# A two-layer expert kernel: the first and last step of layer two on all eight banks, weight sums spread over other ticks, and a fixed order for the matrix engine

## The chip, the cores and the metric

One core of one Trainium2 chip runs the kernel. The metric is the device time of one launch in microseconds (us). The matrix engine is PE, its weight loads PEld; VectorE is DVE, ScalarE ACT, GpSimd POOL, and SP is the engine that issues most DMA transfers.

## The reference

Linear attention feeds a feed-forward layer with ELU (layer one), and that a mixture of four experts with ReLU (layer two). 2304 tokens, width 512, all in float32:

```
kv  = einsum('bhsd,bhse->bhde', k, v);  o = einsum('bhsd,bhde->bhse', q, kv)
x   = o / sqrt(mean(o*o) + 1e-6) * g_norm              # 2304 x 512
h   = x @ w_in;  y = elu(h) @ w_out                    # layer one, 512 -> 2048 -> 512
p   = domain_probs / (sum(domain_probs) + 1e-9)
out = sum over e of p[:, e] * (relu(y @ w1[e]) @ w2[e])   # layer two, 512 -> 1024 -> 512
```

## The kernel before

**Numbers.** w_in and w_out arrive as float64 bit patterns and are turned into float32 on DVE and ACT (`convert`, in five pieces). Every large product is made of three passes: each operand is split into a high part (a cast on ACT, lines 194, 266 and 638) and a low part (a subtraction, line 191 or 271, on POOL or DVE), and PE multiplies high by high, high by low and low by high. A matmul has 128x128 weights and 384 tokens.

**Layer one.** Tokens go in six blocks of 384 (T), hidden units in 16 chunks of 128, taken in the groups 0-1, 2-3, 4-7, 8-11 and 12-15. Group one is computed inside the attention, block by block (index j). One chunk and one block is 12 matmuls into bank `ps_h` (`product1`, lines 481 to 483), ELU (`begin_elu` on ACT, `end_elu` at line 495 on DVE, which frees the bank), a split (`split_h`), and 12 matmuls into the four banks `ps_y` (`product2`, lines 513 to 515), which DVE or ACT adds into `acc` (line 507, line 505). There are two `ps_h` banks, so `product1` of one chunk waits until line 495 has read the chunk two before.

**Layer two.** Tokens go in three pairs of blocks, with four experts each: twelve steps (`moves`). Each step multiplies by blocks 2x2 in Strassen's manner with seven products, P1 to P7: a q half (x by w1) and an m half (hidden by w2), each of 7 products by two slices s, so 14 units of 12 matmuls. q units of step n alternate with m units of step n-1. In the first step there are only q units, and behind the last q unit only m units of the last step. Line 576 is every matmul of both halves. Results lie in four double banks: `qa` and `qb` for q, `ma` and `mb` in turn for m. P2 goes into the bank of P1 and P6 into that of P5 once ACT has copied it (`copy p`, line 692, line 601 for q); DVE adds the banks into sums u and c (lines 604 to 620 and 697 to 713). The hidden blocks are added up (`sums_of_h`, lines 628 to 630), cast (line 638) and lowered (line 191); results are weighted (line 684) and added into `acc` (line 685). At the end of a pair 128x128 transposes on PE turn `acc` (`emit_out`, line 731), ACT copies them and a DMA stores them. Halfway through the last step of a pair `make_forms` adds up the next pair's x blocks (line 327). All the tiles that hold these intermediate results come in turn from one ring of 16 (`small`).

**Weights of layer two.** The 16 quarters of w1 and w2 are loaded in blocks b11 to b22 (`load_block`, line 248), added into t1 to t4 (line 261, DVE), split and written back to memory (`keptw`, line 276). Three tables say at which tick of its quarter each piece starts: `FORMS_SLOW`, `FORMS_FAST` and `FORMS_LATE`; a b entry loads a block of the next quarter, and the number behind the table is the length of a quarter in ticks. Twelve quarters are made during layer one, four in layer two. A tick is one turn of the loop that writes the program, 12 matmuls.

**Order.** The attention runs in a hand-written order on every engine (a place number for each piece; `at_place`). From the last three groups of layer one on, DVE, ACT and POOL run in the order of the program (`in_program_order`), while PE and SP run in the order that a scheduler chose. On SP all loads and stores stand in one queue: a store that waits for its data holds up the loads behind it.

## Time and profile before

| | before |
|---|---|
| median of three runs (lowest to highest) | 1195.65 us (1195.27 to 1197.15) |
| the profiled execution, its own time | 1193.98 us |
| its span in the trace | 1192.2 us |
| PE busy | 1166.6 us, 98% of the span |
| DVE, POOL, ACT busy | 799.4, 676.0, 587.3 us |

The profile is one execution. Its time is 1.67 us below the median, and 1.78 us of it lie outside the span. PE's share is an average over stages, so that the idle time of PE has to be looked for stage by stage: 0 to 115 us attention with group one, to 465 us the other groups of layer one, to 494 us the first step of layer two, from 1148.35 us the m units of the last step.

### The profile page before, as it was taken

The page shows a single profiled execution, that of the slowest core. Times are in us where ns is not written, and L with a number is a line of the kernel's source. Part 1 is how long each engine was busy: PE and PEld are TensorE (multiplying, and loading weights), DVE is VectorE, ACT ScalarE, POOL GpSimd, SP SyncE. Part 2 cuts the span into 40 slices and gives each one's busy share as a digit, 9 for nine tenths or more (in the row PEclk, how much of TensorE's full clock was granted, in tenths as well). Part 3 has the DMA queues.
Part 4 walks back from the last instruction along what each step waited for, and adds up shares of the span by engine and source line. Part 5 has one row for each costly group of instructions (what it writes and reads, how often), then busy time and mean ns, then how long its engine had stood idle before and what let it go on. Part 6 is the DMA issues. An engine that isn't in the chain of part 4 may idle for free.

```text
span 1192.2 us, 18877 instructions
## 1 busy us (share of the span) xinstructions
PE 1166.6 (98%) x7039; PEld 1151.9 (97%) x7039; DVE 799.4 (67%) x945; ACT 587.3 (49%) x937; POOL 676.0 (57%) x526
## 2 busy tenths in 40 slices
PE   9899999999999999999999999999999999999997
PEld 8899999999999999999999999999999999999996
DVE  5877987767776673667687956364758573647485
ACT  3677656666665563544444443434344434343342
POOL 1223457777777693676678954454567544445441
PEclk9999999999999999999999999999999999999999
DMA  9614777668778866999998978888888888888873
GB/s 344 231 44 142 256 262 250 228 219 314 244 219 291 314 249 219 347 332 367 319 352 305 346 245 256 284 252 267 247 274 257 260 265 273 262 259 267 257 242 114
DMA packets 112159, 312.22 MB, mean 262 GB/s; under 512 B 19580, under 2 KB 40644, under 8 KB 110532
## 3 DMA queue, kind: packets, MB, share of 16 engines
q1 hardware_dynamic: 106372, 296.86, 74.4%
q10 hardware_dynamic: 5696, 14.16, 3.3%
q8 instruction: 56, 0.92, 0.3%
q14 instruction: 35, 0.29, 0.1%
HBM read 238.06 MB, written 72.91 MB: 261 GB/s over the span
## 4 chain that ended last, share of the span: by engine, by line
PE 55%; DVE 3%; issue 1%; ACT 0%; POOL 0%; ACTq 0%; DVEq 0%; POOLq 0%
PE ps_qb L576 16%; PE ps_ma L576 15%; PE ps_mb L576 13%; PE ps_qa L576 11%; DVE acc L685 1%; DVE m L684 0%; PE ps_mb L731 0%; DVE h L629 0%; DVE h L191 0%; DVE u L604 0%; DVE h L628 0%; POOL c L707 0%; DVE u L704 0%; DVE f L191 0%; PE ps_ma L731 0%
## 5 line engine op out<-in xcount | busy, mean ns | idle before, releaser
L191 POOL TENSOR_TENSOR h<-h 128x384 fp32r<-128x384 f32 x232 | 284.0, 1250 | 203.8 <-ACT h L638 198.3
L576 PE MATMUL ps_qb<-f,ws 128*128 128x384 f32 x1152 | 216.9, 336 | 4.8 <-DVE u L604 3.7
L576 PEld LDWEIGHTS ps_qb<-f,ws 128*128 128x128 f32 x1152 | 201.1, 188 | 6.1 <-DVE u L604 4.7
L576 PE MATMUL ps_ma<-h,ws 128*128 128x384 f32 x1080 | 200.0, 335 | 0.8 <-DVE h L191 0.7
L191 POOL TENSOR_TENSOR h<-e,h 128x384 fp32r<-128x384 f32 x93 | 107.5, 1157 | 149.1 <-ACT h L194 135.2
L576 PEld LDWEIGHTS ps_ma<-h,ws 128*128 128x128 f32 x1080 | 187.9, 188 | 1.9 <-DVE h L191 1.0
L576 PE MATMUL ps_mb<-h,ws 128*128 128x384 f32 x936 | 173.5, 336 | 1.6 <-ACT o L738 0.8
L638 ACT CAST h<-h 128x768 fp32r<-128x768 f32 x168 | 139.9, 833 | 66.9 <-PE ps_ma L576 35.9
L576 PEld LDWEIGHTS ps_mb<-h,ws 128*128 128x128 f32 x936 | 164.1, 189 | 2.2 <-issue 1.1
L576 PE MATMUL ps_qa<-f,ws 128*128 128x384 f32 x864 | 162.7, 334 | 0.5 <-DVE acc L507 0.5
L576 PEld LDWEIGHTS ps_qa<-f,ws 128*128 128x128 f32 x864 | 150.7, 188 | 1.1 <-DVE acc L507 0.9
L595 ACT ACTIVATE h<-h 128x768 f32<-128x768 f32 x72 | 61.0, 848 | 154.9 <-DVE h L610 73.2
L481 PE MATMUL ps_h<-x,w 128*128 128x384 f32 x384 | 129.7, 338 | 4.7 <-DVE e L495 4.7
L482 PE MATMUL ps_h<-x,w 128*128 128x384 f32 x384 | 128.6, 335 | 0.7 <-DVE x L457 0.7
L515 PE MATMUL ps_y<-h,w 128*128 128x384 f32 x384 | 128.4, 334 | 0.7 <-POOL w L191 0.7
L514 PE MATMUL ps_y<-h,w 128*128 128x384 f32 x384 | 128.4, 334 | 0.2 <-POOL h L191 0.2
L483 PE MATMUL ps_h<-x,w 128*128 128x384 f32 x384 | 128.4, 334 | 0.0
L513 PE MATMUL ps_y<-h,w 128*128 128x384 f32 x384 | 122.2, 336 | 0.2 <-ACT acc L505 0.2
L495 DVE SCALAR_TENSOR_TENSOR e<-e,ps_h 128x384 f32<-128x384 f32 x96 | 52.6, 549 | 68.6 <-ACT e L491 58.0
L271 POOL TENSOR_TENSOR wform<-wform 128x512 fp32r<-128x512 f32 x56 | 81.2, 1458 | 24.1 <-ACT wform L266 17.4
L194 ACT CAST h<-e 128x384 fp32r<-128x384 f32 x96 | 49.0, 511 | 68.0 <-DVE e L495 67.9
L490 ACT ACTIVATE e<-ps_h 128x384 f32<-128x384 f32 x96 | 46.9, 489 | 66.3 <-PE ps_h L483 58.3
(119 smaller groups left out, 1870.8 us busy)
## 6 DMA issues: line engine op xcount, KB each, us to landing
ws<-keptw SPq DMA_DIRECT2D x336, 512.0 KB, 4.5
keptw<-wform SPq DMA_DIRECT2D x112, 512.0 KB, 4.2
wraw<-in_moe_w_dram SPq DMA_DIRECT2D x64, 256.0 KB, 5.5
keptx<-x ACTq DMA_DIRECT2D x6, 1536.0 KB, 6.5
x<-keptx SPq DMA_DIRECT2D x6, 1536.0 KB, 8.6
raw<-in_moe_w_in_dram SPq DMA_DIRECT2D x16, 512.0 KB, 4.2
raw<-in_moe_w_out_dram SPq DMA_DIRECT2D x16, 512.0 KB, 4.4
qkv<-in_k_dram SPq DMA_DIRECT2D x18, 256.0 KB, 5.8
```

The source lines that it names most:

```text
L191: eng.tensor_tensor(out=l, in0=x, in1=h, op=ALU.subtract)
L271: eng.tensor_tensor(out=f[:, 1].bitcast(F32R), in0=src, in1=f[:, 0], op=ALU.subtract)
L481: nc.tensor.matmul(ps, ah, bh, start=(kk == 0), stop=False)
L482: nc.tensor.matmul(ps, ah, bl, start=False, stop=False)
L483: nc.tensor.matmul(ps, al, bh, start=False, stop=(kk == KD - 1))
L495: nc.vector.scalar_tensor_tensor(out=e, in0=e, scalar=-1.0, in1=ps_h.pop((j, c)), op0=ALU.add, op1=ALU.max)
L513: nc.tensor.matmul(ps, bh[:, cols], hi, start=first, stop=False)
L514: nc.tensor.matmul(ps, bh[:, cols], lo, start=False, stop=False)
L515: nc.tensor.matmul(ps, bl[:, cols], hi, start=False, stop=last)
L576: nc.tensor.matmul(ps[:, c, :T], a, x[:, b, kk, :], start=start and kk == 0 and n == 0, stop=stop and kk == 1 and n == 2, skip_group_check ...
L595: nc.scalar.activation(src, src, AF.Relu)
L638: nc.scalar.copy(f[:, 0], src)
```

## The change

**Attention.** The low parts of the first block's h and of the first two chunks of w_out move from POOL to DVE. In block 1 both halves of the first `half` (24 matmuls) stand before the 12 transposes of the next x, where one half stood; the ELU of chunk 0 of block 1 comes later.

**Conversions.** Those of group one come every 3.4 ticks instead of every 3, the later ones start 3 ticks later.

**Weight sums.** Quarters of `FORMS_SLOW` last 12 ticks, not 13, and there are 8 of them, not 7; those of `FORMS_FAST` last 10, not 8, and there are 4, not 5. In the fast table the block b21 of the next quarter is loaded 4 ticks before its use in t4, where it was 2 (from tick 10 to tick 14, where it was 9 to 11). `FORMS_LATE` starts at tick 10, lasts 26.

**Orders.** SP runs in program order in the last three groups, PE in program order in layer two.

**First step.** Its products come as P1 P3 P2 P5 P4 P6 P7 and take the four double banks in turn.

**Small tiles.** Weighted results are multiplied in place instead of into a new tile, and the sums of the last pair's x blocks lie in an `acc` tile that is free by then.

**Last step.** Its 14 m units come in an order of their own, P1 P3 P5 P3 P5 P4 P2 P6 P7 with slices mixed, on all banks. Eight of its operands are split ahead into the place of x blocks that are no longer needed; for slice 1, and for S2 and A22, DVE makes the low parts. The last quarter of the output is transposed and added up on PE: `add_third` multiplies by the identity into a bank, first `acc`, then the weighted last product, in three thirds that ACT copies and SP stores.

```
-    FORMS_SLOW = "t1:0 t2:2 P5:3 t3:4 t4:5 P3:6 b12:7 b11:7 P4:7 ... P6:11 b21:12", 13
-    FORMS_FAST = "t1:0 t2:1 P5:2 t3:2 b12:3 b11:3 b22:3 t4:3 ... P6:9 b21:9", 8
+    FORMS_SLOW = "t1:0 t2:2 P5:3 t3:4 b12:5 b11:5 t4:5 P3:6 P4:7 ... P6:11 b21:11", 12
+    FORMS_FAST = "t1:0 t2:1 P5:2 t3:3 b12:4 b11:4 t4:4 P3:5 b22:5 ... P6:10 b21:10", 10
...
-            d["a"] = double("qa")
+            d["a"] = next_m(ALL) if step == moves[0] else double("qa")
...
-        on_vector = a in ("S2", "A22") or step == moves[-1] and a in ("A12", "S4")
+        on_vector = a in ("S2", "A22") or step == moves[-1] and s and a != "A11"
...
-        m = small("m")
+        m = src if last_use else small("m")
         tt(out=m, in0=src, in1=by, op=ALU.mult)
...
+            transposed = out_part(p, 0, 1)
+            by, t = late["p", step][:, 1, :], small("m")
+            for n, m in enumerate(thirds):
                 tt(out=t[:, :, m], in0=ps[:, :, m], in1=by[:, m].unsqueeze(1).to_broadcast([P, 2, P]), op=ALU.mult)
-                tt(out=a[:, 0:2, m], in0=a[:, 0:2, m], in1=t[:, :, m], op=ALU.add)
-                emit_out(p, 1, 0, n, TT)
+                add_third(n, t, False)
+                o = small("o")
+                copy(o[:, 0, :HK], in_thirds[n])
+                store(o, nc.sync, p, 1, 0, n, TT)
+            o = small("o")
+            nc.vector.tensor_copy(o, transposed)
+            store(o, nc.sync, p, 0, 1)
...
+            nc.tensor.matmul(
+                in_thirds[n][:, c * P:(c + 1) * P], src[:, c, thirds[n]], ident,
+                start=first and c == 0, stop=not first, skip_group_check=True,
+            )
...
-            at_place(z + 13.1, half, j - 1, (2, 3))
+            at_place(z + (13.1 if j > 1 else 9.02), half, j - 1, (2, 3))
-    plan_float32(1, 0, .1, 4.6, 11.42, 11.6, 11.8)
+    plan_float32(1, 0, .1, 4.6, 11.42, 11.6, 11.8, nc.vector)
...
-                at_step(begins + n * (3 if g == 1 else 6), convert, len(rows))
+                at_step(begins + (n * 17 // 5 if g == 1 else 3 + n * 6), convert, len(rows))
...
+    in_program_order(start_order, E_.SP)
...
+    Q_FIRST = [(name, s) for s in (0, 1) for name in ("P1", "P3", "P2", "P5", "P4", "P6", "P7")]
+    M_LAST = [tuple([n[:2], int(n[2])]) for n in "P10 P11 P30 P50 P31 P51 P40 P41 P20 P21 P60 P61 P70 P71".split()]
...
     in_program_order(start_order, E_.DVE, E_.Activation, E_.Pool)
+    in_program_order(second_layer, E_.PE)
```

How the instructions stand, in the engines' own order (a line, an operation, the tile written, the tiles read, the shape, and how many in a row):

PE at the start of layer two, before: the first q units, which use the two q banks.

```order
L576 MATMUL ps_qa<-f,ws 128x384 x12
L576 MATMUL ps_qb<-f,ws 128x384 x12
L576 MATMUL ps_qa<-f,ws 128x384 x12
L576 MATMUL ps_qb<-f,ws 128x384 x12
L576 MATMUL ps_qa<-f,ws 128x384 x12
L576 MATMUL ps_qb<-f,ws 128x384 x24
L576 MATMUL ps_qa<-f,ws 128x384 x12
L576 MATMUL ps_qb<-f,ws 128x384 x12
L576 MATMUL ps_qa<-f,ws 128x384 x12
L576 MATMUL ps_qb<-f,ws 128x384 x12
L576 MATMUL ps_qa<-f,ws 128x384 x12
L576 MATMUL ps_qb<-f,ws 128x384 x12
```

The same place after:

```order
L579 MATMUL ps_qa<-f,ws 128x384 x12
L579 MATMUL ps_ma<-f,ws 128x384 x12
L579 MATMUL ps_qa<-f,ws 128x384 x12
L579 MATMUL ps_qb<-f,ws 128x384 x12
L579 MATMUL ps_mb<-f,ws 128x384 x12
L579 MATMUL ps_qb<-f,ws 128x384 x12
L579 MATMUL ps_qa<-f,ws 128x384 x12
L579 MATMUL ps_ma<-f,ws 128x384 x12
L579 MATMUL ps_qb<-f,ws 128x384 x12
L579 MATMUL ps_ma<-f,ws 128x384 x12
L579 MATMUL ps_mb<-f,ws 128x384 x12
L579 MATMUL ps_qa<-f,ws 128x384 x12
```

The 14 units, which went over two double banks, now go over four; these are the first twelve.

DVE in the last group of layer one, before: one quarter's sums t1 to t4 (the four rows of line 261, t1 first) and ELU ends (line 495); the fourth sum, t4, reads block b21.

```order
L261 TENSOR_TENSOR wform<-wraw 128x512
L495 SCALAR_TENSOR_TENSOR e<-e,ps_h 128x384
L271 TENSOR_TENSOR wform<-wraw,wform 128x512
L261 TENSOR_TENSOR wform<-wraw,wform 128x512
L261 TENSOR_TENSOR wform<-wraw 128x512
L495 SCALAR_TENSOR_TENSOR e<-e,ps_h 128x384
L261 TENSOR_TENSOR wform<-wraw,wform 128x512
L495 SCALAR_TENSOR_TENSOR e<-e,ps_h 128x384
L507 TENSOR_TENSOR acc<-ps_y,acc 128x384 x4
```

The same place after (line 495 is now 498, line 507 is 510):

```order
L261 TENSOR_TENSOR wform<-wraw 128x512
L261 TENSOR_TENSOR wform<-wraw,wform 128x512
L498 SCALAR_TENSOR_TENSOR e<-e,ps_h 128x384
L261 TENSOR_TENSOR wform<-wraw 128x512
L498 SCALAR_TENSOR_TENSOR e<-e,ps_h 128x384
L261 TENSOR_TENSOR wform<-wraw,wform 128x512
L498 SCALAR_TENSOR_TENSOR e<-e,ps_h 128x384
L510 TENSOR_TENSOR acc<-ps_y,acc 128x384 x4
```

An ELU end now stands between t2 and t3, where t2 and t3 followed each other, and the low part (line 271) of the quarter before no longer stands among the four; behind t4 an ELU end still comes next.

PE at the end of the program, before: the m units of the last step on `ma` and `mb`, the transposes (line 731) of the output.

```order
L576 MATMUL ps_mb<-h,ws 128x384 x24
L576 MATMUL ps_ma<-h,ws 128x384
L576 MATMUL ps_mb<-h,ws 128x384 x24
L576 MATMUL ps_ma<-h,ws 128x384 x23
L731 MATMUL ps_mb<-ident,acc 128x128 x6
L576 MATMUL ps_ma<-h,ws 128x384 x24
L576 MATMUL ps_mb<-h,ws 128x384 x4
L576 MATMUL ps_ma<-h,ws 128x384 x24
L576 MATMUL ps_mb<-h,ws 128x384 x20
L731 MATMUL ps_ma<-ident,acc 128x128 x6
L576 MATMUL ps_mb<-h,ws 128x384 x24
L731 MATMUL ps_ma<-ident,acc 128x128 x8
L731 MATMUL ps_mb<-ident,acc 128x128 x4
```

The same place after (line 576 is now 579, 731 is 766; line 748 is `add_third`; a unit that reads `f` has its operand in a place of the x blocks):

```order
L579 MATMUL ps_ma<-f,ws 128x384 x24
L579 MATMUL ps_mb<-f,ws 128x384 x12
L766 MATMUL ps_qa<-ident,acc 128x128 x6
L579 MATMUL ps_mb<-h,ws 128x384 x12
L766 MATMUL ps_ma<-ident,acc 128x128 x6
L579 MATMUL ps_qb<-f,ws 128x384 x12
L748 MATMUL ps_mb<-ident,acc 128x128 x4
L748 MATMUL ps_qa<-ident,acc 128x128 x2
L579 MATMUL ps_qb<-h,ws 128x384 x12
L766 MATMUL ps_ma<-ident,acc 128x128 x6
L748 MATMUL ps_mb<-ident,m 128x128 x4
L748 MATMUL ps_qa<-ident,m 128x128 x2
```

The units use four double banks, three groups of six transposes stand between units, and the last six matmuls are those that add the last product's thirds.

## Rows read from the trace of the kernel before

**Rows 1.** Windows, whole core: stretch, its length, busy us (instructions) by engine, PE clock, DMA.

```profile
400.00:465.00 65.00, 60.74 (x344) 59.16 (x342) 43.56 (x57) 36.96 (x71) 50.30 (x40) 1.00 0.74 267
692.00:1148.35 456.35, 455.59 (x2644) 454.58 (x2644) 264.95 (x244) 184.30 (x232) 238.46 (x190) 1.00 0.83 262
1148.35:1192.20 43.85, 34.21 (x193) 31.36 (x192) 30.69 (x35) 14.59 (x20) 10.65 (x9) 0.99 0.48 154
```

**Rows 2.** Timeline, PE in attention and behind it: start, us, operation, [idle before, releaser].

```profile
47.33 0.44 PE L515 MATMUL ps_y<-h,w 128*128 128x384 f32 x1 [0.74 <-POOL w L191]
...
49.68 1.85 PE L446 MATMUL ps_xT<-ident,sq 128*128 128x128 f32 x12 [1.39 <-DVE sq L435]
...
158.34 0.44 PE L481 MATMUL ps_h<-x,w 128*128 128x384 f32 x1 [0.80 <-DVE e L495]
```

**Rows 3.** Waits of PE, whole span: who for whom, total us, times, longest.

```profile
PE ps_h L481 <- DVE e L495: 4.7, 6, 1.6
```

**Rows 4.** Timeline, last group of layer one, DVE and PE.

```profile
400.40 0.69 DVE L261 TENSOR_TENSOR wform<-wraw,wform 128x512 f32<-128x512 f32 x1 [6.00 <-DMA wraw<-in_moe_w_dram]
...
435.87 1.83 DVE L261 TENSOR_TENSOR wform<-wraw,wform 128x512 f32<-128x512 f32 x1 [3.56 <-DMA wraw<-in_moe_w_dram]
...
438.23 0.44 PE L481 MATMUL ps_h<-x,w 128*128 128x384 f32 x1 [1.55 <-DVE e L495]
```

**Rows 5.** Timeline, PE in layer two's first step, 12 matmuls a row.

```profile
478.91 2.38 PE L576 MATMUL ps_qb<-f,ws 128*128 128x384 f32 x12 [1.11 <-DVE h L610]
481.13 2.24 PE L576 MATMUL ps_qa<-f,ws 128*128 128x384 f32 x12
483.21 2.24 PE L576 MATMUL ps_qb<-f,ws 128*128 128x384 f32 x12
...
488.16 2.38 PE L576 MATMUL ps_qb<-f,ws 128*128 128x384 f32 x12 [0.63 <-DVE u L604]
```

**Rows 6.** Timeline, ACT's copy p and PE, and a window, at pair ends.

```profile
563.54 0.80 ACT L692 COPY p<-ps_mb 128x768 f32<-128x768 f32 x1 [3.32 <-PE ps_mb L576]
...
683.58 0.80 ACT L692 COPY p<-ps_mb 128x768 f32<-128x768 f32 x1 [2.58 <-DVE acc L685]
...
684.41 2.39 PE L576 MATMUL ps_qb<-f,ws 128*128 128x384 f32 x10 [2.34 <-DVE u L604]
...
685.90:689.30 3.40, 3.40 (x13) 3.40 (x12) 3.40 (x4) 0.88 (x2) 0.20 (x1) 0.50 0.55 188
...
922.94 1.34 PE L576 MATMUL ps_qb<-f,ws 128*128 128x384 f32 x6 [0.76 <-DVE u L604]
```

**Rows 7.** Line 692, all 24 copies p: what ended ACT's idle time before, us, times.

```profile
  PE ps_ma L576: 20.1, 13
  PE ps_mb L576: 12.8, 7
```

**Rows 8.** Timeline, DVE beside POOL and DVE alone.

```profile
1144.16 1.86 POOL L616 TENSOR_TENSOR h<-u,p 128x768 f32<-128x768 f32 x1
...
1144.26 2.58 DVE L684 TENSOR_TENSOR m<-c,p 128x768 f32<-128x768 f32 x1 [0.99 <-POOL c L707]
...
1154.65 0.94 DVE L191 TENSOR_TENSOR h<-h 128x768 fp32r<-128x768 f32 x1
```

**Rows 9.** Timeline of the last step and, last, the DMA view of 1140 to 1192.2.

```profile
1164.40 0.85 PE L731 MATMUL ps_mb<-ident,acc 128*128 128x128 f32 x6 [1.43 <-DVE acc L685]
...
1186.88 0.41 PE L731 MATMUL ps_ma<-ident,acc 128*128 128x128 f32 x2 [1.22 <-DVE acc L721]
...
1187.60 0.37 ACT L740 COPY o<-ps_mb 128x256 f32<-128x256 f32 x1 [1.10 <-PE ps_mb L731]
...
1188.40 0.37 ACT L740 COPY o<-ps_ma 128x256 f32<-128x256 f32 x1 [0.42 <-ACT o L740]
...
1189.65 0.34 ACTq L742 DMA_DIRECT2D out_dram<-o  x1
...
out_dram<-o ACTq DMA_DIRECT2D x3, 384.0 KB, 2.6
```

More of the change, by code (lines that the diff above doesn't have):

```diff
@@ L330, in make_forms @@
         other = nc.vector if p else nc.gpsimd
-        if p:
+        if p > 1:
+            t = acc_p.tile([P, KD, T], F32, tag=f"acc{2 * p - 2}", name="s")
+            two = [t[:, 2 * n:2 * n + 2] for n in (0, 1)]
+        elif p:
             two = [late["s"].tile([P, 2, T], F32, tag="s", name="s") for _ in range(2)]
@@ L654, in load_p, with next_m, in_last @@
         )
-    def next_m():
+    def next_m(of=("ma", "mb")):
         turns["m"] = turns.get("m", 0) + 1
-        return double("ma" if turns["m"] % 2 else "mb")
+        return double(of[turns["m"] % len(of)])
+    ALL = ("mb", "qa", "ma", "qb")
+    def in_last(what):
+        a, c = ("ma", "mb") if turns["m"] % 2 else ("mb", "ma")
+        return double({"P1": a, "P3": "qa", "P5": c, "P4": "qb", "P7": "qb", (1, 1): "qa", (0, 0): a, (0, 1): a,
+                       "sums": c, "sum": "qa"}[what])
     def emit_m(u, step, name, s):
```

111 lines of the change are left out of this document (65 added, 46 removed).

## The prediction

> **What bounds the kernel now.** I read the windows first: they tell in which stage PE is not full. From 692 to 1148.35 us PE is busy 455.59 of 456.35 us, while DVE, ACT and POOL have room [rows 1]. PE is the bound there, and its number of large matmuls does not change, so nothing is to be won. The idle time lies in a few places: 4.26 us in the last group of layer one (60.74 busy of 65.00) and 9.64 us in the last step (34.21 of 43.85) [rows 1], the rest in single waits. I read the waits of PE next, and the timeline at each. A wait of PE delays the end by its own length only if no later wait absorbs it; since PE is the engine that ends last through nearly the whole program, each wait taken away counts in full, unless the same wait comes later. So the sum is one of waits, each at its place.
>
> **Attention.** The wait of 0.74 us for POOL's low part of a weight goes, since that split moves to DVE, and so does most of the 1.39 us for line 435: 24 matmuls instead of 12, so 2.1 us more of work, stand ahead of the transposes [rows 2]. That is 2.1 us. Against it: the second half's two banks must be emptied by ACT first, and the matmuls that used to stand behind the transposes no longer cover the copy of the transposed x. The trace does not show either wait; the nearest rows are the two just named, 0.74 and 1.39, and I put the two new waits together between 0.1 and 2.6. I take 1.1, near the middle, since both wait for an operation that already runs: a gain of 1.0, from -0.5 to 2.0. The conversions that come at wider distance take the ELU end at 158.34 out of their way, a wait of 0.80 [rows 2]. I take 0.5 of it, from 0 to 0.8.
>
> **Last group of layer one.** Six waits of `product1` for line 495 make 4.7 us, 0.80 of them at 158.34 [rows 2, 3], so 3.9 us are left. Why is line 495 late? DVE runs in a fixed order, and right ahead of that ELU end stands the weight sum of line 261, which waits for its DMA: 6.00 us at 400.40, 3.56 at 435.87 [rows 4]. The ELU end behind it frees the bank, and PE waits 1.55 at 438.23 [rows 4]. The block it waits for was loaded two ticks ahead (2 x 2.08, from the spacing of 481.13 and 483.21 [rows 5], is 4.2 us). After, it is four ticks, 8.3 us; the two waits together with two ticks ask for up to 10.2 us in one case and 7.7 us in the other, but the load was behind stores on SP's queue, and fewer quarters (four fast ones of 10 ticks, not five of 8) put fewer stores there. DVE may still wait 1.9 us at the first place, which the ELU end then shows to PE in part. The sum of those waits falls to about a quarter: gain 3.0, from 1.0 to 3.7. The cost is more weight work in the groups before, where PE has no idle time: quarters of 12 ticks instead of 13 raise POOL's and DVE's share by a twelfth, and the window of the last group, the fullest, has POOL at 50.30 of 65.00 [rows 1], so I put nothing there, up to 0.5 of new waits.
>
> **First step.** The waits of 1.11 and 0.63 at 478.91 and 488.16 are each for DVE to empty the one bank that comes again after one unit [rows 5]. With four double banks there are at least two units, 4.2 us, between the last product of a bank and its next use by another. In place products have one unit, 2.08 us, for ACT's copy, which takes 0.80 and starts some 0.2 us after PE's last matmul [rows 6]. So both waits go: 1.7, from 1.1 to 1.74.
>
> **Pair ends.** At 684.41 PE waits 2.34 us. DVE works through a sum there, ACT's copy p starts after 2.58 us of idle time that DVE's `acc` ended, and the ring of 16 small tiles is what joins them [rows 6]. Right behind the wait the granted clock is 0.50 from 685.90 to 689.30, that is 1.2 instead of 2.4 GHz: 3.4 us that do the work of 1.7 [rows 6]. So that wait costs 4.0 in all. In the changed order the same DVE operations stand ahead of that copy, and the m product in place needs the copy right behind, so I expect 2.5 us and the same clock: 0, from -0.2 to 4.0. At 922.94 the wait of 0.76 [rows 6] is for the copy that no longer waits for a tile, since the last pair's sums have one of their own and weighted results are multiplied in place. 0.76 go; from 0 to 0.76.
>
> **Pinned order on PE.** q and m units now alternate strictly. A P2 or P6 follows its P1 or P5 with one unit of the other half between: 2.08 us against the copy's 0.2 + 0.80, a slack of 1.08. ACT sat idle until PE was done before 20 of the 24 copies [rows 6, 7], so it has nothing queued there that would be late. The scheduler of before could put other matmuls in; now a late copy shows. Cost: 0.5, from 0 to 1.5. The order of SP in layer one is not a cost of its own beyond the last group's term.
>
> **Last step.** Before, from 1148.35, there are 43.85 us [rows 1]. After: 14 units of 2.08 are 29.1 us. Two groups of six transposes and the first six of `add_third` stand between units, 0.6 each (the row says 0.85 for six, of which some 0.25 is the pipeline's end that a following matmul covers [rows 9]): 30.9. Then DVE weights the first third, 0.4, PE adds it, 0.41 [rows 9], and with 0.4 of hand-overs ACT's first copy starts at 32.2. From the first copy to the end of the span it is 4.6 us in before (1187.60 to 1192.2), with copies 0.80 apart [rows 9]. That stays; the part of 384 KB that SP issues last adds one issue, 0.35, and its landing of 2.6 is longer than that of a third by an estimated 0.9. That gives 32.2 + 5.8 = 38.0, a gain of 5.8. It holds only if DVE keeps up, since it makes six of the low parts of slice 1. Alone such an operation takes 0.94; beside POOL 2.58 [rows 8]. The first that PE needs is S2 of slice 1, four units (8.3 us) into the step. Its chain is one eviction, two sums, a cast (I put it at 0.85, near copy p's 0.80 [rows 6]) and the split: 4 x 0.94 + 0.85, with four hand-overs of 0.15 5.2 us. Three of these read two operands of SBUF; I let each be held up by half of the excess of 2.58, about 0.8, as the upper end: 7.7. So it arrives in time, and by the same count the others have more room: S1 at 7.9 against 10.4, S3 at 9.6 against 14.6, A12 at 11.4 against 18.7. Its bounds: 4.3, if waits of 1.43 and 1.22 as at 1164.40 and 1186.88 [rows 9] come back at half their size, and 7.0, if the large store lands first.
>
> The row at 1144.26 shows DVE starting 0.1 us after a POOL operation of 1.86 and needing 2.58, 1.64 more than alone [rows 8]. The Trainium skill, "SBUF — State Buffer", section "SBUF: two separate sides", makes a rule of it: VectorE with two SBUF inputs and a GpSimd operation that reads SBUF take turns on one port pair, held for the whole instruction, and the later one waits it out. That rule speaks against moving splits to DVE while POOL still has its own; by it all three operations could lose the 1.64 of the row, S2 would come at 10.1, PE would wait 1.8, and the step would take 39.8 in place of 38.0. I stay with 38.0, since POOL's low parts for this step are mostly made ahead; the 1.8 lies inside the bounds above and is where D begins.
>
> **Sum.** 1.0 + 0.5 + 3.0 + 1.7 + 0 + 0.75 - 0.5 + 5.8 = 12.25. The profiled execution of before, 1193.98, becomes 1181.7. It stands 1.67 below the median of 1195.65; on the median that is 1183.4, given as 1183.5. All best terms together (without the clock) make 16.0, that is 1179.6; all worst ones, with 0.5 for the fuller middle groups and 1.5 for the pinned order, make 3.7, that is 1192.0.
>
> **Rivals.** *A: layer one gives nothing back.* The loads still come late, because SP's stores wait for POOL, and the attention's new waits eat the old ones: 12.25 less 1.0, 0.5 and 3.0 is 7.75, that is 1187.9. For it speaks that SP's fixed order puts every store ahead of the load that follows it in the program; against it the four ticks. *B: the wait at 684 vanishes too,* if two fewer tiles in the ring let ACT's copy start with PE as in 563.54 [rows 6]: another 4.0, 1179.4. Against it: the tile is still one that DVE's `acc` gives back. *C: the pinned order makes the kernel slower.* Its place is the in-place product: two per step in the eleven steps in which q and m alternate, 22 places. To eat 12.75 us and end at no change each must lose 0.58 us, which means that copy p starts 1.08 + 0.58 = 1.7 us later than in before, two operations of ACT later. From there on it is slower; at 2.0 us later 22 x 0.92 = 20 us are lost, and the time is 1203. Rows 7 speak against it: ACT had been waiting for PE at 20 of 24. *D: the gains are given back.* The waits taken away in the last step return as waits for DVE, which has 30.69 us busy in 43.85 [rows 1] and must be done in 38: then the last step gains at most 1, layer one nothing, and 2.5 to 4 in all are left, some 1192; or, with the pinned order at its 1.5, no change.
>
> **How the numbers follow.** Forecast (1181 to 1186.5) 0.62; A 0.17; B 0.10; D 0.07, of which 0.04 within 0.2%; C 0.04, of which 0.03 slower. The range leaves out C, D and the far end of B: 1179 to 1190. 0.2% is 2.4 us, about what a measurement of this kernel can tell from no change. Faster by more: 0.62 + 0.17 + 0.10 + 0.03 = 0.92, with a point given to what I have not seen: 0.91. Same 0.05, slower 0.04.
>
> **What would show it.** Right: the window of the last step is about 38 us and PE has no wait over 0.7 in it but for the thirds; the waits of line 481's place for the ELU end make less than 1.5 in all; none in the first step behind its first unit; a wait of about 2.5 us with half the clock still near 680. Wrong: waits of PE on copy p all through layer two (C), DMA waits of DVE in the last group as long as before (A), waits for low parts in the last step (D).

## The result, and the profile after

The changed kernel takes 1182.36 us in the median of four runs (1181.64 to 1184.94), the kernel before 1196.35 (four runs, 1195.27 to 1197.15). The ratio is 0.9888, with a 95% interval of 0.9869 to 0.9906: faster by 1.1%. The forecast was 1183.5, in a range of 1179.0 to 1190.0.

The profiled execution of the changed kernel is the longest of its four, 1184.94 us with a span of 1183.2. Its windows, in the places that answer to [rows 1] (stretch, its length, busy us by engine, PE clock, DMA share, GB/s):

```profile
398.00:463.00 65.00, 63.02 (x360) 62.06 (x360) 41.23 (x56) 37.73 (x72) 49.48 (x40) 1.00 0.76 269
690.00:1143.97 453.97, 453.87 (x2634) 452.96 (x2633) 255.95 (x245) 185.25 (x234) 240.80 (x196) 1.00 0.81 263
1143.97:1183.20 39.23, 34.37 (x211) 33.78 (x210) 26.57 (x31) 9.58 (x14) 3.16 (x2) 0.96 0.54 169
```

In the last group PE's idle time falls from 4.26 to 1.98 us, in the last step from 9.64 to 4.86; the last step takes 39.2 us, not 43.85. What PE still waits for, from the view of waits (who for whom, total us, times, longest):

```profile
PE ps_ma L579 <- ACT p L705: 2.1, 1, 2.1
PE ps_h L484 <- DVE e L498: 1.8, 4, 0.8
...
PE ps_kv L386 <- DMA qkv<-in_v_dram: 1.3, 2, 0.8
...
PE ps_mb L579 <- DMA ws<-keptw: 0.8, 1, 0.8
```

The first is the wait at the first pair's end that was forecast to stay (it answers to 684.41 in [rows 6]). The second is what is left of [rows 3]. The other two are new: a late load of v at the start, and a late load of weights in layer two.

A sum of waits is a little short of what they cost, since the shown idle time begins where the modelled end of the last matmul lies, not where the next could have started: at 158.34 in before 0.80 us is shown, while from start to start it is 1.13 us where two matmuls in a stream are 0.17 apart, so that the wait costs 0.96. So I compare lengths from one marker to the next. The markers are the first matmul of the attention's output (13.66 us in before), the `product1` that waits 0.2 us at 110.05, the first unit of layer two (465.05), the first unit that belongs to the last step (1148.35) and the end of the span. The last column says where PE's granted clock was 0.50 for 3.4 us (a fall behind PE's last matmul left out).

| run | to first output | to the 110 marker | to layer two | to the last step | last step | half clock at |
|---|---|---|---|---|---|---|
| before | 13.66 | 96.39 | 355.00 | 683.30 | 43.85 | 686 |
| changed | 15.50 | 96.26 | 350.34 | 681.87 | 39.20 | 16, 682 |
| changed, again (e11) | 15.14 | 95.45 | 350.30 | 680.71 | 39.20 | none |
| e1, an addition in the wrong step | 14.11 | 94.80 | 350.35 | 680.80 | 39.20 | 678 |
| e2, PE's order free | 15.04 | 95.10 | 350.34 | 682.99 | 39.19 | none |
| e3, tables of before | 13.87 | 94.82 | 354.73 | 680.51 | 39.19 | 418 |
| e4, attention of before | 13.80 | 97.85 | 350.34 | 683.00 | 39.20 | 51, 682 |
| e5, early addition | 15.00 | 96.34 | 350.35 | 680.34 | 39.19 | 15 |
| e6, late table of before | 14.60 | 94.98 | 350.36 | 682.79 | 39.20 | 680 |
| e7, first step of before | 14.09 | 96.30 | 350.36 | 682.93 | 39.20 | 15 |
| e8, thirds | 14.07 | 96.33 | 350.33 | 681.96 | 38.82 | 15 |
| e9, early addition, S3 later, thirds | 14.20 | 94.64 | 350.35 | 678.34 | 38.83 | none |
| e10, as e9, SP in program order | 14.88 | 96.29 | 350.32 | 680.21 | 38.84 | 15 |
| e12, low parts on POOL | 14.69 | 95.24 | 350.31 | 683.43 | 39.33 | 682 |

Two columns repeat within 0.1 us wherever the code is the same: 350.3 for layer one, 39.2 for the last step. The gain is 4.7 us in each of them. The first column differs by up to 1.8 us between kernels that have the same first instructions in the same order, since the loads of v land earlier or later; it stands for no change. The stretch to the last step differs between executions of the same code too: a half clock costs it some 1.6 us, and waits for weight loads come and go. e11 has one wait at 566.13 that the changed kernel's first profile lacks, at a unit that in e4, e5 and e8 waits for weights:

```profile
566.13 2.35 PE L579 MATMUL ps_qb<-f,ws 128*128 128x384 f32 x12 [0.95 <-ACT h L641]
```

So a difference of about 1 us in this column, between one execution and another, proves nothing without the waits that make it.

### The profile page after: what moved, and what is told of

Its sections match the earlier page's. It is cut to its first block, busy times and chain, and to the rows that moved or that the text cites. A ratio compares the mean times of both kernels' runs of the same rounds, so it can differ in the third digit from the quotient of the medians.

```text
span 1183.2 us, 18890 instructions
## 1 busy us (share of the span) xinstructions
PE 1166.8 (99%) x7057; PEld 1156.2 (98%) x7057; DVE 777.2 (66%) x946; ACT 583.0 (49%) x936; POOL 669.0 (57%) x523
## 4 chain that ended last, share of the span: by engine, by line
PE 88%; DVE 4%; ACT 3%; DMA 2%; POOL 2%; issue 1%; SPq 0%; ACTq 0%; POOLq 0%; DVEq 0%
PE ps_qb L579 15%; PE ps_mb L579 15%; PE ps_ma L579 12%; PE ps_qa L579 11%; PE ps_h L484 5%; PE ps_h L485 5%; PE ps_h L486 5%; PE ps_y L516 5%; PE ps_y L518 5%; PE ps_y L517 5%; PE ps_o L405 1%; DMA ws<-keptw 1%; POOL h L191 1%; POOL wform L271 1%; DVE x L460 1%
## 5 line engine op out<-in xcount | busy, mean ns | idle before, releaser
L191 POOL TENSOR_TENSOR h<-h 128x384 fp32r<-128x384 f32 x222 | 258.9, 1193 | 191.4 <-ACT h L641 185.7
L579 PE MATMUL ps_qb<-f,ws 128*128 128x384 f32 x1116 | 210.1, 336 | 0.0
L579 PEld LDWEIGHTS ps_qb<-f,ws 128*128 128x128 f32 x1116 | 195.4, 189 | 0.1
L579 PE MATMUL ps_mb<-h,ws 128*128 128x384 f32 x1032 | 193.0, 334 | 0.8 <-DMA ws<-keptw 0.8
L579 PEld LDWEIGHTS ps_mb<-h,ws 128*128 128x128 f32 x1032 | 180.0, 188 | 1.1 <-DMA ws<-keptw 1.1
L579 PE MATMUL ps_ma<-h,ws 128*128 128x384 f32 x852 | 160.4, 336 | 2.3 <-ACT p L705 2.1
L579 PE MATMUL ps_qa<-f,ws 128*128 128x384 f32 x852 | 159.5, 335 | 0.6 <-DVE acc L510 0.5
L579 PEld LDWEIGHTS ps_ma<-h,ws 128*128 128x128 f32 x852 | 149.1, 188 | 3.6 <-ACT p L705 3.2
L641 ACT CAST h<-h 128x768 fp32r<-128x768 f32 x160 | 133.3, 833 | 21.8 <-PE ps_mb L579 8.7
L619 POOL TENSOR_TENSOR h<-u,p 128x768 f32<-128x768 f32 x24 | 52.1, 2169 | 51.9 <-DVE u L617 30.5
```

What stands on the lines that cost most here:

```text
L191: eng.tensor_tensor(out=l, in0=x, in1=h, op=ALU.subtract)
L579: nc.tensor.matmul(ps[:, c, :T], a, x[:, b, kk, :], start=start and kk == 0 and n == 0, stop=stop and kk == 1 and n == 2, skip_group_check ...
L641: nc.scalar.copy(f[:, 0], src)
```

## The experiments

All are the changed kernel with the edit shown, unless said otherwise; "..." marks lines left out. e1 to e4 ran on one chip, e5 to e12 on another. The kernel before, measured beside them, had medians of 1196.39 us (e1 to e4), 1195.29 (e5 to e8) and 1195.34 (e9 to e12). The 95% intervals of all twelve against before overlap that of the changed kernel (0.9869 to 0.9906), so that no single edit is told from the changed kernel by its time alone. The readings below rest on the traces, one profiled execution of each.

**e1: an addition moved, one step too late.**

```
...
-            after(7 if step == moves[-2] else 1, into_out, step, c, 1, 0)
+            after(7 if step == moves[-2] else 1, into_out, step, c, 1, 0, 0 if step == moves[E - 1] else 1)
```

The lines left out are the `if wait` lines that e5 shows.

> The changed kernel with one more edit: in the last step of the first pair the last weighted product is added into acc at once, not two DVE operations later. Theory: PE's wait of 2.11 us at 680.64 comes from the small tile that ACT's copy p needs and that this addition gives back behind two unrelated DVE sums (1.76 and 1.77 us). Then that wait and the half clock behind it (about 1.7 us) both go, the wait for copy p is no longer in the trace, and the time falls by 3.5 to 4.2 us against the changed kernel (1182.4), to about 1178.5. Rival: DVE is simply full there, and PE meets the next late operation instead (an eviction of q or S2): a wait of 1 us or more stays within 680 to 690, the clock still falls, and the gain is under 1 us.

Measured: 1183.94 us (1180.40 to 1184.36), and the wait is there as before, 2.11 us, with half clock at 678. The edit missed: the addition that copy p waits for belongs to the third step, `moves[E - 2]`, which ends while the fourth begins. So e1 says nothing on the theory; it serves as another run of nearly the changed kernel. e5 has the edit at the right step.

**e2: PE's order left to the scheduler.**

```
-    in_program_order(second_layer, E_.PE)
```

> The changed kernel without the fixed order on PE in layer two. Theory of the prediction (fixed order costs about 0.5 us, from 0 to 1.5): time within 1.5 us of the changed kernel, 1181 to 1183, the middle stretch of layer two up to 0.5 us shorter. Rival: the fixed order is part of the gain, because the scheduler puts units of the last step ahead of operands that come late; then the last step is 1 us or more longer than 39.2, and the time is 1183.5 or more.

Measured: 1184.48 us (1182.58 to 1184.64). The theory does not hold; of its rival, that the fixed order is part of the gain does, but not the place. The last step is as long as with the fixed order, 39.19, but the stretch ahead of it takes 682.99 us against 680.71 in e11, both without half clock: 2.3 us more. PE's timeline shows where:

```profile
486.62 2.35 PE L579 MATMUL ps_ma<-f,ws 128*128 128x384 f32 x12 [0.90 <-ACT h L610]
489.48 2.15 PE L579 MATMUL ps_qb<-f,ws 128*128 128x384 f32 x11 [0.51 <-DMA ws<-keptw]
517.55 2.32 PE L579 MATMUL ps_qb<-f,ws 128*128 128x384 f32 x12 [0.45 <-DMA ws<-keptw]
570.77 2.35 PE L579 MATMUL ps_mb<-h,ws 128*128 128x384 f32 x12 [0.80 <-DMA ws<-keptw]
681.41 1.16 PE L579 MATMUL ps_qb<-f,ws 128*128 128x384 f32 x5 [2.21 <-DVE u L607]
918.09 2.35 PE L579 MATMUL ps_qb<-f,ws 128*128 128x384 f32 x12 [0.71 <-DVE u L607]
```

The wait at the second pair's end (0.76 in [rows 6]) is back, and a wait of 0.90 in the first step. In both places the scheduler lets a q unit go earlier than the fixed order does, and its bank is not empty yet: in the first step P7 comes right behind P2 in the same bank `ma`, which ACT (line 610) has to empty, where the fixed order has P6 between; at 918.09 a q unit goes ahead of an m unit, and DVE (line 607) has not emptied `qb`. The waits for weights, 1.76 us together, are as much as e11's two at 566.13 and 569.30 (0.95 and 0.81), so the 2.3 us are those of the order. With the changed first step and the small tiles in place the fixed order is a gain, where the prediction had a cost. By the medians it can't be seen: e1, nearly the changed kernel and measured beside e2, has 1183.94.

**e3: the tables of before.**

```
...
+    FORMS_SLOW = "t1:0 t2:2 P5:3 t3:4 t4:5 P3:6 b12:7 b11:7 P4:7 P7:8 P1:9 b22:9 P2:10 P6:11 b21:12", 13
+    FORMS_FAST = "t1:0 t2:1 P5:2 t3:2 b12:3 b11:3 b22:3 t4:3 P3:4 P4:5 P7:6 P1:7 P2:8 P6:9 b21:9", 8
...
+        at = plan_forms(n, at, FORMS_SLOW if n < 7 else FORMS_FAST, lambda hh, step: at_step(hh, *step))
```

> The changed kernel with the slow and fast tables of weight sums of before (13 ticks for seven quarters, 8 for the rest), SP's order still fixed. Theory: the later spacing of block b21 is what saves in the last group: DVE waits 3 us or more for its DMA again at two places, the waits of PE for the ELU end rise from 1.8 to 4 us or more, the time from 1182.4 to about 1185. Rival: SP's fixed order alone had done it; then those waits stay under 2.5 us and the time within 1 us of 1182.4.

Measured: 1185.55 us (1184.91 to 1188.79). Layer one takes 354.73 us, 4.4 more than with the new tables and nearly what before takes. DVE's waits from 390 to 462 us, first of e3, then of the changed kernel:

```profile
DVE e L498 <- ACT e L494: 15.7, 9, 3.6
DVE wform L261 <- DMA wraw<-in_moe_w_dram: 5.8, 2, 5.5
DVE wform L261 <- issue: 5.2, 1, 5.2
```

```profile
DVE e L498 <- ACT e L494: 23.6, 9, 5.5
DVE acc L510 <- PE ps_y L518: 2.4, 1, 2.4
```

With the old tables line 261 waits 5.8 us for its block and 5.2 us more before the sum at 416.80; behind that stands an ELU end, and PE waits:

```profile
418.41 0.69 PE L484 MATMUL ps_h<-x,w 128*128 128x384 f32 x1 [2.52 <-DVE e L498]
```

From 418.4 the clock is 0.50 for 3.4 us. 2.5 us of wait, 2.7 from start to start, and some 1.6 of lost clock make the 4.4. With the new tables line 261 has no wait for a DMA at all. SP's fixed order is in both, so the tables are what saves in the last group, as the theory said; of its two places with a wait of 3 us or more for a DMA the profile names one (5.5) and gives no cause for the other (5.2). The conversions are as changed in both, and no run undoes them.

**e4: the attention of before.**

```
...
-            at_place(z + splits, split_h, j, c, nc.gpsimd if j else nc.vector)
+            at_place(z + splits, split_h, j, c, nc.gpsimd)
...
-            at_place(z + (13.1 if j > 1 else 9.02), half, j - 1, (2, 3))
+            at_place(z + 13.1, half, j - 1, (2, 3))
...
-    plan_float32(1, 0, .1, 4.6, 11.42, 11.6, 11.8, nc.vector)
...
+    plan_float32(1, 0, .1, 4.6, 11.42, 11.6, 11.8)
...
```

> The changed kernel with the attention of before (splits on POOL, one half ahead of the transposes, ELU places). Theory: the waits of 0.7 for POOL's low part of the weight and of 1.4 for line 438 come back and the 0.61 for the transposed x goes: 1 to 2 us longer, 1183.5 to 1184.5. Rival: what was won there is lost before the attention's end (waits of 0.2 at 94 to 112 take it up), and the time is the same within 0.5 us.

Measured: 1185.68 us (1183.96 to 1186.18). The two waits are back, as long as in before within 0.01 us:

```profile
47.48 0.44 PE L518 MATMUL ps_y<-h,w 128*128 128x384 f32 x1 [0.73 <-POOL w L191]
49.83 2.44 PE L449 MATMUL ps_xT<-ident,sq 128*128 128x128 f32 x12 [1.39 <-DVE sq L438]
```

Its stretch to the 110 marker is 97.85 us, of which some 1.6 are half clock right behind these waits; without that it is about that of before, 96.39, which has the same waits. The new attention takes 94.6 to 95.5 in the seven executions without half clock there. So it saves 0.9 to 1.8 us; the theory holds for the stretch, its rival falls. The median lies above the 1184.5 that it allowed; this execution has two half clocks.

**e5: the addition moved at the right step.**

```
-            after(7 if step == moves[-2] else 1, into_out, step, c, 1, 0)
+            after(7 if step == moves[-2] else 1, into_out, step, c, 1, 0, 0 if step == moves[E - 2] else 1)
...
-        after(wait, lambda: tt(out=a, in0=a, in1=m, op=ALU.add))
+        if wait:
+            after(wait, lambda: tt(out=a, in0=a, in1=m, op=ALU.add))
+        else:
+            tt(out=a, in0=a, in1=m, op=ALU.add)
```

> The changed kernel, and the last weighted product of the third step of the first pair is added into acc at once, ahead of two unrelated DVE sums (line 327 and line 632). In the first experiment the same edit stood one step too late. Theory: that addition gives back the tile that copy p at 680 waits for; with it about 3.5 us earlier PE's wait of 2.11 us goes whole, and with it the half clock that follows in most executions: the stretch from layer two's first unit to the last step's first is 2.1 to 4.0 us shorter than in the changed kernel (681.9, and 680.8 in the first experiment). Rival: DVE is full there and the next late operation (the eviction of line 607, or S2) stops PE for 1 us or more at 676 to 690; the gain is under 1 us.

Measured: 1179.40 us (1178.65 to 1183.04); against before 0.9870 (0.9849 to 0.9891). The wait falls from 2.11 to 1.09 us, no half clock follows, and what is left has another cause:

```profile
675.33 1.65 DVE L701 TENSOR_TENSOR acc<-acc,c 128x768 f32<-128x768 f32 x1
...
676.90 1.77 DVE L327 TENSOR_TENSOR s<-acc 128x768 f32<-128x768 f32 x1
...
678.70 0.83 ACT L321 CAST f<-s 128x768 fp32r<-128x768 f32 x1 [4.16 <-DVE s L327]
679.44 0.79 ACT L708 COPY p<-ps_ma 128x768 f32<-128x768 f32 x1
...
680.28 2.02 PE L579 MATMUL ps_ma<-h,ws 128*128 128x384 f32 x10 [1.09 <-ACT p L708]
```

The addition ends at 676.98, about when PE is done with the bank, and copy p could start some 0.2 us later. But ACT has the cast of the next form ahead of it, and that now waits 4.16 us for line 327, which the addition has pushed back. So the tile was the cause of half of the wait, and the rival is half right too: DVE is full, and copy p hangs on both operations, on the addition by its tile and on line 327 by ACT's order. The stretch, 680.34 us, is only 1.5 shorter than in the changed kernel and 0.4 than in e11, where 2.1 to 4.0 was expected.

**e6: the late table of before.**

```
+    FORMS_LATE = "t1:0 t2:4 P5:5 t4:8 P3:9 t3:12 P7:13 b12:14 P4:16 P1:18 P2:20 P6:22 b11:22 b22:25 b21:25", 28
...
-    at = 10
+    at = 4
```

> The changed kernel with the late table of weight sums of before (starts at tick 4, 28 ticks a quarter). New in the changed kernel is that PE waits 0.6 to 0.8 us for a weight load at 570. Theory: on SP's queue that load stands behind a store that waits for POOL and two block loads, because the quarters now come every 26 ticks from tick 10; with the old table the wait goes and the stretch from the first unit of layer two to the last step is 0.5 to 1 us shorter, unless DVE's sums in the first step stop PE again. Rival: the loads are late because PE's fixed order asks for them earlier; then a wait for weights of 0.3 us or more stays near 515 to 575.

Measured: 1183.08 us (1182.51 to 1183.73). The wait for weights at 570 is gone, but three others are there, 0.67 at 498.35, 0.48 at 501.19 and 0.88 at 508.55, together 2.0 us. The waits move with the table, but do not go. So the table is not the cause by itself. The rival is ruled out by e2: with PE's order free the wait at 570 is still there, 0.80 us.

**e7: the first step of before.**

```
-    Q_FIRST = [(name, s) for s in (0, 1) for name in ("P1", "P3", "P2", "P5", "P4", "P6", "P7")]
+    Q_FIRST = [(name, s) for s in (0, 1) for name in Q_ORDER]
...
-            d["a"] = next_m(ALL) if step == moves[0] else double("qa")
+            d["a"] = double("qa")
```

> The changed kernel with the first step of layer two as before (order P1 P3 P2 P5 P6 P4 P7 on two banks), PE's order still fixed. Theory: waits for DVE's evictions of 1.1 and 0.6 us come back within 25 us of the first unit, and the stretch to the last step is 1.7 to 2.3 us longer. Rival: the later start of the late weight sums alone keeps DVE free there; then both stay under 0.3 us and the length is that of the changed kernel.

Measured: 1185.88 us (1184.67 to 1188.42). The stretch to the last step is 682.93 us against 680.71 in e11, both without half clock there: 2.2 us, as long as the theory said. The waits are 0.93 and 0.89:

```profile
470.30 2.35 PE L579 MATMUL ps_qb<-f,ws 128*128 128x384 f32 x12 [0.93 <-ACT p L604]
486.02 2.37 PE L579 MATMUL ps_qb<-f,ws 128*128 128x384 f32 x12 [0.89 <-ACT p L604]
```

They are now for ACT's copy ahead of a P6, which in this order follows its P5 without a unit between when PE may not choose. In before it was DVE's eviction [rows 5]. So e7 has the two banks of before, but not its waits, and prices them under the fixed order; with the free order of before they cost the 1.11 and 0.63 of [rows 5].

**e8: another order for the last thirds.**

```
-        in_thirds.extend((a[:, 0, :HK], a[:, 1, :HK], b[:, 0, :HK]))
+        in_thirds.extend((a[:, 0, :HK], b[:, 0, :HK], a[:, 1, :HK]))
...
-                store(o, nc.sync, p, 1, 0, n, TT)
+                store(o, nc.scalar if n == 1 else nc.sync, p, 1, 0, n, TT)
...
```

> The changed kernel with the output's last thirds in another order of banks (first and second third in different banks) and the second third stored from ACT's queue, so that SP issues three stores, not four. Theory: the last step's 39.2 us (5.8 predicted to be saved, 4.65 measured) hold 0.46 us of wait for ACT's copy and a last store of 384 KB that is issued 0.6 us behind the others; the last step becomes 38.3 to 38.8. Rival: the end is set by the landing of the 384 KB store alone, whose source DVE writes after the thirds; then it stays at 39.0 or more.

Measured: 1182.12 us (1180.40 to 1183.31); the last step is 38.82 us, 0.38 shorter, at the edge of what was expected. The wait of 0.46 us for ACT's copy is gone. That is too little to see in the time. The order of banks and the store's queue were changed together, so their shares stay open.

**e9: e5 and e8 together, and the form S3 one slot later.**

```
-        for slot in (5, 6, 8, 10, 12, 14, 15, 17):
+        for slot in (5, 6, 8, 10, 12, 14, 15 if n else 16, 17):
```

> The changed kernel with three edits: the early addition into acc of the fifth experiment, the fourth form of the second pair (S3) one slot later, so that ACT's cast of it no longer stands ahead of copy p, and the thirds of the eighth experiment. Theory: of the 1.09 us that were left at 680 ACT's cast behind a DVE sum was the whole cause; the wait is now under 0.3 us and no half clock follows there, so the stretch from layer two's first unit to the last step is 678 to 679.5, the last step 38.8, and the time 3 to 4.5 us under the changed kernel of the same call. Rival: S3's later low part stops PE at its P4 unit (0.5 us or more near 690), and the gain stays at that of the early addition.

Measured: 1179.80 us (1178.14 to 1181.71); against before 0.9870 (0.9852 to 0.9888). The stretch to the last step is 678.34 us and the last step 38.83, both as expected (38.8); at the pair's end PE has one wait left:

```profile
682.01 2.38 PE L579 MATMUL ps_qb<-f,ws 128*128 128x384 f32 x12 [0.28 <-ACT p L604]
```

By the trace it is 2.7 us shorter than e11 without any help from the clock (2.37 and 0.37 in the two stretches), and the medians of the two, measured beside each other, differ by 2.5 (1182.28 and 1179.80), under the 3 to 4.5 that were expected. Of the 2.37 the pair's end makes some 1.9 (2.11 less 0.28 of shown wait); e9 also lacks e11's wait of 0.95 at 566.13, which is not the edit's doing. The two intervals against before overlap, so the gain over the changed kernel rests on the lengths in the trace more than on the times.

**e10: as e9, with SP in program order in layer two and the stores a tick later.**

```
-    in_program_order(second_layer, E_.PE)
+    in_program_order(second_layer, E_.PE, E_.SP)
...
-            after(1, keep, name, f)
+            after(1 if n < IN_LAYER1 else 2, keep, name, f)
```

> As e9, and SP runs in program order in layer two as well, with the stores of weight sums one tick later. Theory: the waits for weights (0.4 to 1.3 us at 514, 567 and 570 in several executions) come from a store that waits for POOL's low part on SP's queue ahead of the loads; in program order, one tick later, the low part is made by then, the waits fall under 0.3 us each, and the time is 1 to 2 us under e9. Rival: SP's scheduler-made order had loads up to six units ahead; in program order they are four ahead, land in 8 to 9 us when the queues are full, and PE waits for weights more often: 1 us or more over e9.

Measured: 1182.34 us (1180.74 to 1183.09), 2.5 more than e9. The wait at 567 is gone, but PE waits 1.21 us for weights at 679.55 and 1.06 for DVE at 517.41. The rival is right in the main: PE waits 1.9 us for weights where e9 has 0.8, and the shortest time from a load's issue to the unit that uses it falls from 7.5 to 5.6 us. The wait for DVE is not explained by it, and the later stores, changed together with the order, may have a share.

**e11: the changed kernel again.**

> The changed kernel itself, beside the others on the same chip, for comparison: 1181 to 1184.

Measured: 1182.28 us (1179.77 to 1184.49).

**e12: the last step's low parts on POOL.**

```
-        on_vector = a in ("S2", "A22") or step == moves[-1] and s and a != "A11"
+        on_vector = a in ("S2", "A22") or step == moves[-1] and a in ("A12", "S4")
```

> The changed kernel with the low parts of the last step's hidden operands on the engines of before (POOL for S1 and S3, DVE for A12, S4, S2 and A22 of both slices). Theory: the last step's gain is made by the order of the products, the four banks and the operands split ahead, not by DVE: POOL's low part of S1 for slice 1 comes some 6.6 us into the step and PE asks for it at 10.4, so the last step stays within 0.4 us of 39.2. Rival: POOL is late with it, since it has the forms of other operands queued; PE waits 0.7 us or more in the last step, which then takes 40 us or more.

Measured: 1183.06 us (1179.99 to 1184.79). The last step is 39.33 us, 0.13 longer; PE has no wait for a low part. POOL does some 6.3 us of work in it and is in time. So the last step's gain is not made by moving low parts from POOL to DVE; which engine splits matters by a tenth. What is left are the order of the products, the four banks, the operands split ahead and the output's thirds on PE. No run undoes these one by one. The trace shows what they do together: ahead of ACT's first copy of the thirds PE waits six times in before, 5.3 us in all, at 1164.40 and 1186.88 [rows 9] and at

```profile
1153.56 4.45 PE L576 MATMUL ps_mb<-h,ws 128*128 128x384 f32 x24 [0.71 <-ACT p L692]
1160.76 2.21 PE L576 MATMUL ps_ma<-h,ws 128*128 128x384 f32 x11 [0.67 <-DVE h L191]
1178.89 0.85 PE L731 MATMUL ps_ma<-ident,acc 128*128 128x128 f32 x6 [0.46 <-DVE acc L685]
1180.58 4.43 PE L576 MATMUL ps_mb<-h,ws 128*128 128x384 f32 x24 [0.85 <-ACT o L738]
```

In the changed kernel it has no wait there. The length up to that copy falls by 6.0 us (39.25 to 33.25), and 1.4 of it are given back behind the copy (4.6 to 6.0).

## Why the prediction was right, and where its steps were not

The time, 1182.36, lies 1.1 us under the forecast, and the sum of 12.25 us is near the measured difference of the medians, 14.0. The profiled executions differ by 9.0 us; that of the changed kernel had a start 1.8 us later and one more stretch of half clock. Against e11 it is 11.4. That the sum came so near is in part luck: layer one gave more than its terms, the last step less, and a gain that was entered as a cost was eaten by waits that the sum did not have. The terms:

| term | forecast | measured | how |
|---|---|---|---|
| attention | 1.0 | 0.9 to 1.8 | 96.39 less the executions without half clock; e4 |
| conversions | 0.5 | 1.5 | the same 401 matmuls from the 110 marker on: 71.13 (110.05 to 181.18), then 69.62 (111.76 to 181.38); no run undoes it |
| last group | 3.0 | 3.2 | the rest of 355.00 less 350.3; e3 |
| first step | 1.7 | 1.7 of shown waits gone; 2.2 with PE's order fixed | [rows 5]; e7 less e11 |
| wait at 684 | 0 | 0.2 of wait, clock by chance | 2.34 to 2.11 |
| wait at 922 | 0.75 | gone, but by PE's order | e2 |
| fixed order of PE | -0.5 | +2.3, with the one above and part of the first step | e2 less e11 |
| last step | 5.8 | 4.65 | 43.85 less 39.20 |
| waits for weights | not in it | -0.6 to -2.6 | 570.07 and its like, e1 and e8 |

The terms of layer two's middle must not be added up: e7 and e2 each undo one edit with the other in place, and both count waits in the first step. As lengths, with 1.6 us for each half clock taken out, the stretch falls from 681.7 to 680.3 us in the changed kernel and 680.7 in e11: 1.0 to 1.4 in all, where the sum had 1.95 (1.7 + 0.75 - 0.5).

**Conversions and last group.** The step of the last group was right, and so was its size: DVE's wait for block b21 held up the ELU end. The wait of 6.00 us [rows 4] is gone whole, not to 1.9 us. But two waits in [rows 3] were never of that kind: at 407.18 the changed kernel still waits 0.64 us, as before (0.67 at 407.75), since two sums of x blocks (line 327) stand ahead of the ELU end on DVE, and at 401.05 it still waits 0.81 us, with DVE idle until ACT's exponential:

```profile
400.44 0.55 DVE L498 SCALAR_TENSOR_TENSOR e<-e,ps_h 128x384 f32<-128x384 f32 x1 [5.51 <-ACT e L494]
...
401.05 0.44 PE L484 MATMUL ps_h<-x,w 128*128 128x384 f32 x1 [0.81 <-DVE e L498]
```

ACT itself waits 4.42 us for PE there. PE runs two `product1` one behind the other and then has nothing to do until the ELU of the first is through. Of the 1.30 us that stood there in before, DVE's DMA made 0.5. A wait with one name had two causes, and the later one hid the other. So the waits of line 484's place make 1.8 us in all, where less than 1.5 was given as a sign of being right. What was sized too low is the term of the conversions, 1.5 us and not 0.5: the wait at 158.34 went whole, not half of it, it cost 0.96 and not the 0.80 shown, and 0.4 us of smaller delays at 140 and 154 went with it.

**Pinned order.** This step failed. It looked only at what a fixed order can lose (a copy that is late) and not at what the scheduler's order was already losing. The 22 places of rival C cost nothing: the view of waits has copy p once, at 680. In e2 the free order costs 2.3 us, in the first step and at the second pair's end. The rival also counted only the m half's products in place; the q half has them too, and in e7 it is one of those, behind its P5 without a unit between, that stops PE. With the step the reason for the 0.76 at 922 falls too: the prediction put it down to the tile that copy p no longer waits for. In e2 the tiles are the new ones, copy p starts right behind PE, and the wait of 0.71 us is there, for DVE's u, which empties the bank `qb`. It is the order that takes it away.

**The pair's end.** Forecast as 2.5 us with half clock, it is 2.11 us, with half clock in the profiled execution. The reason given, that DVE's addition holds the tile of copy p, held: e5 takes it away and half of the wait goes. The other half stays because DVE has two operations there of 1.7 us each, and copy p needs both, one by its tile and one because ACT casts a form first; e9 moves the form, and 0.28 us are left.

**Last step.** The size was off by 1.15 us. The changed kernel's rows, PE's, DVE's, ACT's and SP's, in time:

```profile
1148.84 0.96 DVE L191 TENSOR_TENSOR h<-h 128x768 fp32r<-128x768 f32 x1 [0.90 <-ACT h L641]
...
1172.36 1.05 PE L748 MATMUL ps_mb<-ident,acc 128*128 128x128 f32 x8
1173.25 0.61 PE L748 MATMUL ps_qa<-ident,acc 128*128 128x128 f32 x4
1173.61 2.34 PE L579 MATMUL ps_qb<-h,ws 128*128 128x384 f32 x12
1175.79 0.82 PE L766 MATMUL ps_ma<-ident,acc 128*128 128x128 f32 x6
1176.47 0.71 PE L748 MATMUL ps_mb<-ident,m 128*128 128x128 f32 x4
...
1177.22 0.37 ACT L735 COPY o<-ps_mb 128x256 f32<-128x256 f32 x1 [5.95 <-PE ps_mb L748]
...
1177.62 2.49 SPq L780 DMA_DIRECT2D out_dram<-o  x4
...
1177.64 0.71 PE L748 MATMUL ps_mb<-ident,m 128*128 128x128 f32 x4 [0.46 <-ACT o L735]
```

The six matmuls of `add_third` stand in the trace as twelve (8 and 4) and keep PE from 1172.36 to 1173.61, 1.25 us, where the sum had the 0.6 of six transposes. They are plain matmuls, not transposes, and each is recorded twice. A third group of six transposes, which the sum lacks, stands ahead of the thirds (1175.79 to 1176.47); it covers the 0.4 that the sum gave DVE for weighting. With the thirds' two each, which take 0.71 instead of 0.41, the first copy starts at 1177.22, that is 33.25 us into the step, not 32.2. From there to the end it is 6.0, where 5.8 was forecast, with SP's four stores issued from 1177.62 to 1180.11. The low parts on DVE came in time: that of S2 of slice 1 ends 5.8 us into the step, and PE's units run without a wait up to the thirds. The length of its chain was not right: from the eviction at 1142.09 it takes 7.7 us, not 5.2, since DVE has two other operations in between, and it comes in time because it begins 1.9 us ahead of the step. The sum had put the risk there; e12 says that there was none either way. By the Trainium skill, "SBUF — State Buffer", section "SBUF: two separate sides", each of three operations could have been held up by POOL; the trace shows that for one of them, the sum of line 632 with 1.65 us in place of 0.94, since POOL has only two instructions in this stretch. The rule agrees with the row; it is the number of POOL's instructions that made it harmless.

**What was missing.** PE now waits for weights in layer two, where the waits of before show none: 0.82 us at 570.07, up to 2.6 in all in e8. SP's timeline shows what stands ahead of the load, with the store's issue at 560.63:

```profile
557.54 0.51 SPq L558 DMA_DIRECT2D ws<-keptw  x1
560.63 0.32 SPq L276 DMA_DIRECT2D keptw<-wform  x1
561.00 0.49 SPq L248 DMA_DIRECT2D wraw<-in_moe_w_dram  x1
561.58 8.02 SPq L558 DMA_DIRECT2D ws<-keptw  x6
```

The store waits 2.4 us for POOL's low part, and the weights' load of 561.58 stands behind it and a block load. It lands at 570.03, and PE goes on at 570.07. The loads issued from 561 to 568 us need 8.0 to 9.0 us to land, where the median of all is 4.4. The prediction asked of every moved instruction whether its data come in time, but not of the loads that SP issues behind them. e2 shows that PE's fixed order does not make them, e6 and e10 moved them and did not remove them. Which of the edits brought them, and which order of SP would take them away, is open.

**The rivals.** A (layer one gives nothing back) fell: its three terms came whole, as e3 and e4 show for two of them by undoing them. B (the wait at 684 vanishes) did not come by itself; e9 makes it come, for some 1.9 us, and the clock besides where it would have fallen. C fell, and what took its place has the other sign. D fell: DVE has 26.57 us of work in the 39.2 of the last step and holds up no unit.

## What to carry to other kernels

When an order is fixed by hand, price both what it forbids and what the free order is losing now: the waits of the trace that have a unit of another stream ready behind them are its gain. A wait that names one producer can have a second cause that ends at nearly the same time; take the first away on paper and ask which instruction then stands ahead of the late one on its own engine. For a queue that carries loads and stores, list behind every store that waits for an engine the loads that PE needs next.

## What the runs showed of the hardware that was not expected

**The clock after a wait.** Ten executions have a wait of 2.10 to 2.21 us at the first pair's end. In five of them (the changed kernel, e1, e4, e6, e12) the granted clock was 0.50 for 3.4 us right behind it, in five (e2, e3, e7, e8, e11) it stayed at 1.00. The windows of 3.41 us that begin at 681.98 in the changed kernel and in e11 show both:

```profile
681.98:685.39 3.41, 3.41 (x12) 3.41 (x11) 3.41 (x4) 0.21 (x1) 0.33 (x1) 0.50 0.84 328
```

```profile
681.98:685.39 3.41, 3.41 (x22) 3.41 (x21) 3.38 (x5) 0.98 (x2) 0.00 (x0) 1.00 0.62 216
```

12 matmuls against 22: about 1.7 us. The prediction took the fall of before as part of the wait's price; it is part of it about half of the time. Similar falls came at 15 us behind the late loads at the start, in five of thirteen executions of changed kernels. This is part of the 3 to 5 us by which runs of one kernel differ here, and a reason to compare lengths of stretches, with the clock beside them. It is not all: two of e11's executions have a mean granted clock of 1.000 and differ by 2.8 us (1182.61 and 1179.77).

**Plain matmuls by the identity.** Six of 128x128 in float32 take 1.25 us (1172.36 to 1173.61), twice the 0.57 that six transposes take in the same step (1166.85 to 1167.42); the trace records two matmuls for each.
